# A gated mix of memory attention and GeGLU: the output and the other branch sent through DRAM scratches

## The chip, the cores and the metric

One core of a Trainium2 chip. The metric is the device time of one execution in microseconds, the median over the runs. TensorE (PE) multiplies, ScalarE (ACT), VectorE (DVE) and GpSimd (POOL) move and transform, SyncE (SP) issues nearly all DMAs, which sixteen DMA engines carry out.

## What is computed

Two branches over the same shape, 2048 rows of 640 columns in bf16, mixed by a gate computed from the first branch's input.

```python
def _A_ref(x, mem0, Wq, Wk, Wv, Wo, seg_len):      # 32 heads of 192, M = 8, seg_len = 32
    mem = mem0
    for s in range(n_seg):                          # 64 segments, one after the other
        xs = x[:, s*seg_len:(s+1)*seg_len, :]
        h = jnp.concatenate([mem, xs], axis=1)      # 40 rows
        q, k, v = (jnp.einsum('btd,dhe->bhte', h, W) for W in (Wq, Wk, Wv))
        p = _softmax(jnp.where(mask, q @ k.T * scale, -1e9))
        o = jnp.einsum('bhte,hed->btd', p @ v, Wo)
        mem = o[:, :M, :]                           # the next segment's memory
        outs.append(o[:, M:, :])

def _B_ref(x, w_gate, w_up, w_down):                # 640 -> 1536 -> 640
    return (gelu(x @ w_gate) * (x @ w_up)) @ w_down

g = sigmoid((A_x * gate_w).sum(-1))
out = g * _A_ref(...) + (1 - g) * _B_ref(A_x, ...)
```

## The kernel before

The kernel first computes the whole of the other branch (`_B_ref`) in four blocks of 512 rows, the feed-forward phase. `ffn_down` evacuates each 128 rows into a buffer `brow` and stores them in a DRAM tensor `b_scr` (L878), as rows of 640 columns. At the same time `x_stage` lays the transposed input out in DRAM, and the attention weights are loaded.

Then come the 64 segments in order, each an unrolled list of items (`PROG`, `PROG1`, `PROG3`): `("g", i, k)` are projections, `("tq", o)`/`("tk", o)` transposes, `("sc", o)`, `("ex", o)`, `("pt", o)` scores, softmax and its transposition, `("pv", o)` the product with V and `("wo", o, h)` the output projection. `o` is one of four octets of heads. The place `q = s % 4` of a segment in its group `g = s // 4` decides which list it takes. Every segment works on its 24 rows of x that have no part in the next memory together with the 8 rows of memory; the segment's last 8 rows, the "left" rows, are worked on for four segments at a time (`LQ`, `LK`, `Vl`, `Wb`).

The weights don't all fit. Thirteen pieces of Q, K and V (each 128 partitions of 3072 bytes) and three of Wo (3840 bytes) share their places with a partner: as soon as the first octet's piece was used, `swap_loads` issues the DMA (L635) for the partner that the last octet needs later in the same segment. The next segment goes over the octets in the other order, so every segment swaps once more.

All DMAs of the segment phase are in SP's one stream, in the order in which the items add them, and SP waits for a DMA's conditions before it goes on to the next. The ones that matter here:

- `out_store(s - 1)` (L1029) writes the mixed 32 partitions x 4 column blocks of the segment before, buffer `bz`, to the output. At place 0 it is added at `("g", 0, KT-2)`, ahead of the rest of the K swaps and of the V swaps; at the other places at `("g", 1, KT-1)`, behind the V swaps.
- `x_load(s + 1)` (L743) follows it at `("g", 1, KT-1)`.
- `bz_load(s)` (L1018), after `("wo", 0, 1)`, loads this segment's 32 rows of the other branch into the same buffer `bz`, as four column blocks of 160 columns one below the other. It waits for the output store's landing.
- `mix(s)` multiplies `bz` by one minus the gate on GpSimd (`mix1`, L1085), and VectorE adds the gated attention output (`mix2`, L1087).
- `stg_load` (L1005) brings the left rows' Q and K back from `left_qk_scratch` for the next segment, and one more swap, a Q piece, is added next to it after `("pv", 2)`.
- The left rows of the output and of the other branch have their own buffer `bzl`: `bzl_load` (L1024) and `outl_store` (L1072), once in a group and in eight DMAs each, four at `("g", 1, KT-1)` and four at `("pv", 2)`.

The patterns of the load and of the store put the column block first:

```python
e.dma_start(bz, b_scr[L * s:L * s + L, :].rearrange("t (j n) -> j t n", j=4))
e.dma_start(out2[L * s:L * s + L, :].rearrange("t (j n) -> j t n", j=4), bz)
```

The last segment has no `bz`; `end_load` reads its rows of `b_scr`, and `end_store` writes them.

Of the kernel before, what the change touches and what calls it, by code (L numbers as in the profile page):

```python
# [6 lines left out]
BF = mybir.dt.bfloat16  # L7
# [231 lines left out]
def _build(nc, A_x, A_mem0, A_Wq, A_Wk, A_Wv, A_Wo, seg_len, w_gate, w_up, w_down,  # L239
           gate_w, out, opts=None):  # L240
    opts = dict(opts or {})
    Bsz, S, Dm = A_x.shape
    M = A_mem0.shape[1]
    H, Dh = A_Wq.shape[1], A_Wq.shape[2]
    Df = w_gate.shape[1]
    L = int(seg_len)
    assert Bsz == 1 and M == 8 and L == 32 and Dh == 192
    assert Dm % 128 == 0 and H % 4 == 0 and S % 128 == 0 and Df % 128 == 0
    KT = Dm // 128
    DJ = Dm // 4  # L250
# [32 lines left out]
    g_scr = nc.dram_tensor("gate_scratch", (M, NSEG), F32, kind="Internal").ap()  # L283
# [154 lines left out]
    bz, bzl = [bview(wsB_off[nm], DJ * 2) for nm in ("bz", "bzl")]  # L438
# [8 lines left out]
    LROW = ((3, 4), (0, 3))  # L447
    r_bzlj = [[sreg(wsB_off["bzl"], DJ * 2, 32 * j, 32 * j + M), sreg(wsB_off["bzl"], DJ * 2, 32 * j + M, 32 * j + 32)] for j in range(4)]
# [3 lines left out]
    r_bz, r_bzl = [sreg(wsB_off[nm], DJ * 2) for nm in ("bz", "bzl")]  # L452
# [36 lines left out]
    brow = [bview(ffn_off["brow"] + b * Dm * 2, Dm * 2) for b in range(NBR)]  # L489
    r_brow = [sreg(ffn_off["brow"] + b * Dm * 2, Dm * 2) for b in range(NBR)]  # L490
# [183 lines left out]
    def load_residents(cls, pick=lambda key: True):  # L674
        for key in first:
# [7 lines left out]
           reads=[r_ident], writes=[r_ident])  # L683
# [10 lines left out]
    for i in range(2):  # L694
# [3 lines left out]
               reads=[r_elw], writes=[r_elw])  # L698
# [152 lines left out]
    def ffn_down(blk):  # L851
        n1 = min(Dm, 512)
        for a in range(FA):
            xb = 3 + 2 * (a % 2)
            yb = xb + 1
            wr = [r_ps[xb]] + ([r_ps[yb]] if Dm > 512 else [])
            fns = []
            for f in range(FT):
                if a == 0 and f == FT - 1:
                    S_.add("pe", fns, reads=[r_wd] + r_hT[:f], writes=wr, name="ffn down %d %d" % (blk, a))  # L860
                    fns = []
                fns.append(lambda e, f=f, a=a, xb=xb: e.matmul(ps[:, xb, 0:n1], hT_sb[:, f, a * 128:(a + 1) * 128], wd_sb[:, f, 0:n1],  # L862
                                                               start=(f == 0), stop=(f == FT - 1)))
                if Dm > 512:
                    fns.append(lambda e, f=f, a=a, yb=yb: e.matmul(ps[:, yb, 0:Dm - 512], hT_sb[:, f, a * 128:(a + 1) * 128], wd_sb[:, f, 512:Dm],
                                                                   start=(f == 0), stop=(f == FT - 1)))
            S_.add("pe", fns, reads=[r_wd] + r_hT, writes=wr, name="ffn down %d %d" % (blk, a))
            bs = a % NBR
            S_.add("act", lambda e, bs=bs, xb=xb: e.activation(out=brow[bs][:, 0:n1], in_=ps[:, xb, 0:n1], func=ACTF.Copy),
                   reads=[r_ps[xb]], writes=[r_brow[bs]], name="ffn b evac")  # L870
            if Dm > 512:
                S_.add("dve", lambda e, bs=bs, yb=yb: e.tensor_copy(out=brow[bs][:, 512:Dm], in_=ps[:, yb, 0:Dm - 512]),
                       reads=[r_ps[yb]], writes=[r_brow[bs]], name="ffn b evac2")
            if blk + 1 < NFB:
                for r in range(2 * a, min(2 * a + 2, NGR)):
                    gate_part(blk + 1, r)
            row0 = blk * FB + a * 128
            S_.add(AUXQ, lambda e, bs=bs, row0=row0: e.dma_start(b_scr[row0:row0 + 128, :], brow[bs]),  # L878
                   reads=[r_brow[bs]], writes=[Rg("dr", row0, row0 + 128)], dma_sem="bw%d" % bs, watch=True,
                   name="b store %d" % row0)  # L880

    warm(14)
    ffn_transposes(0)
# [3 lines left out]
    for blk in range(NFB):  # L887
        if blk:
            x_stage(blk)
        ffn_gu(blk)  # L890
        if blk == 0:
            chain_init()
        if blk + 1 < NFB:
            ffn_transposes(blk + 1)
        if blk + 2 < NFB:
            ffn_x_load(blk + 2)
        if blk + 1 == NFB:
            load_residents(1, lambda key: key not in loaded.values())
        ffn_down(blk)
        if blk + 2 == NFB:  # L900
            load_residents(1, lambda key: res_off[key] >= ffn_off["xr"] and res_off[key] + piece_size(key) <= ffn_off["xT"])
        if blk == 0:
            x_load(0)
            xl_load(0)
            xl_load(1)
            x_copy(0)
# [96 lines left out]
    def stg_load(s, h):  # L1003
        lo = (h + s) % 2 * 2
        S_.add(AUXQ, lambda e: e.dma_start(stg_half[h].rearrange("p (o w) -> p o w", o=2), qkl[NOCT * (s // 4) + lo:NOCT * (s // 4) + lo + 2].rearrange(  # L1005
            "o p (q w) -> p q o w", q=4)[:, s % 4]),
               reads=[Rg("qk", NSEG * i + s, NSEG * i + s + 1) for i in (lo, lo + 1)],
               writes=r_stgh[h], dma_sem="stg%d" % h, name="stg s%d %d" % (s, h))
# [6 lines left out]
               name="Kl s%d o%d" % (s, o))  # L1015

    def bz_load(s):
        S_.add(AUXQ, lambda e: e.dma_start(bz, b_scr[L * s:L * s + L, :].rearrange("t (j n) -> j t n", j=4)),  # L1018
               reads=[Rg("dr", 128 * (s // 4), 128 * (s // 4) + 128)], writes=[r_bz], dma_sem="bz", name="bz load s%d" % s)

    def bzl_load(g, js):
        for j in js:
            for n, (lo, hi) in enumerate(LROW):
                S_.add(AUXQ, lambda e, j=j, n=n, lo=lo, hi=hi: e.dma_start(  # L1024
                    bzl[32 * j + M * n:32 * j + M * (n + hi - lo)], rows(b_scr, g)[1][lo:hi, :, DJ * j:DJ * (j + 1)]),
                    reads=[Rg("dr", 128 * g, 128 * g + 128)], writes=[r_bzlj[j][n]], dma_sem="bzl%d" % (2 * j + n), name="bzl load g%d" % g)

    def out_store(s):
        S_.add(AUXQ, lambda e: e.dma_start(out2[L * s:L * s + L, :].rearrange("t (j n) -> j t n", j=4), bz),  # L1029
               reads=[r_bz], writes=[Rg("do%d" % j, s, s + 1) for j in range(4)], dma_sem="outs", watch=True, name="out s%d" % s)  # L1030

    assert r_XLg[1].lo == r_XLg[0].hi and KT * 64 == DJ * 2
    bzx = bview(wsA_off["XLg"], 4 * DJ)
# [4 lines left out]
    r_gx = sreg(wsA_off["xs"], 8)  # L1038

    def end_rows(ap, h, x, lo, hi):  # L1040
        v = ap[L * lo:L * hi, 2 * DJ * h:2 * DJ * (h + 1)]
        return v[0:XA] if x == 0 else v.rearrange("(s t) d -> s t d", t=L)[:, XA:L, :]

    def end_load():
# [24 lines left out]
    def outl_store(g, js):  # L1069
        for j in js:  # L1070
            for n, (lo, hi) in enumerate(LROW):
                S_.add(AUXQ, lambda e, j=j, n=n, lo=lo, hi=hi: e.dma_start(  # L1072
                    rows(out2, g)[1][lo:hi, :, DJ * j:DJ * (j + 1)], bzl[32 * j + M * n:32 * j + M * (n + hi - lo)]),
                    reads=[r_bzlj[j][n]], writes=[Rg("do%d" % j, 4 * g + lo, 4 * g + hi)], dma_sem="outl%d" % (2 * j + n), watch=True, name="outl g%d" % g)

    omg = fview(wsA_off["stats"] + 64, 8)
    r_omg = sreg(wsA_off["stats"] + 64, 8)
# [384 lines left out]
    def segment(s):  # L1462
# [3 lines left out]
        for n, item in enumerate(PROGS[q]):  # L1466
# [210 lines left out]
```

## Time and profile before

| | |
|---|---|
| Median of 3 runs | 1651.54 us (1647.38 to 1653.57) |
| Span of the profiled execution | 2114.2 us |
| The profiled execution's own time | the page gives none beside the span |
| Mean granted TensorE clock in it | 0.654 |
| Busy PE / DVE / ACT / POOL | 2098.0 / 1005.8 / 792.9 / 553.3 us |
| DMA packets | 275415, 499.28 MB |

The profiled execution is longer than the timed ones. Windows are in microseconds from the first instruction; the feed-forward phase lasts to about 264 us, the segments from there on. The DMA share is the mean over the sixteen engines. A row of the timeline has the start, the duration, the engine and the line; SPq is SP's stream of DMA issues, whose duration is the issue's and not the transfer's.

### The profile page before, as it was taken

Reading aid. Unit: us, or ns where it says so; the run is one execution under the profiler, and the core shown is the slowest. Engines: PE = TensorE matmul, PEld = TensorE weight load, DVE = VectorE, ACT = ScalarE, POOL = GpSimd, SP = SyncE. Lnnn points to the kernel's source line nnn. Section 1 sums busy time; section 2 is a strip of 40 time slices with the busy share of each in tenths; the row PEclk is TensorE's granted clock in tenths of the full one; section 3 lists DMA queues with packets and bytes.
Section 4 is the critical chain, followed back from the end, with each engine's and each line's share of the span. In section 5 each row is a group of like instructions: output and inputs, shape, how many; then the busy total and the mean of one; then the engine's idle time right before and its main releaser. Section 6 shows DMA issues by size and latency. Waiting matters only on the chain.

```text
span 2114.2 us, 75845 instructions
## 1 busy us (share of the span) xinstructions
PE 2098.0 (99%) x37107; PEld 958.1 (45%) x28147; DVE 1005.8 (48%) x3039; ACT 792.9 (38%) x1890; POOL 553.3 (26%) x1625
## 2 busy tenths in 40 slices
PE   9999999999999999999999999999999999999997
PEld 3444344444444444444444444444444444444444
DVE  4233254554545454545545454545455454545453
ACT  1111244343434343444434343434444343434342
POOL 1000023232232223232222323232322223222332
PEclk6666666666666666666666666666666666666666
DMA  9612577776768777677767677776777676777775
GB/s 319 182 33 57 184 268 260 248 270 232 253 219 275 244 258 241 227 255 254 274 233 249 221 268 249 255 251 225 248 256 270 239 258 212 261 256 249 254 264 174
DMA packets 275415, 499.28 MB, mean 236 GB/s; under 512 B 121119, under 2 KB 136327, under 8 KB 275079
## 3 DMA queue, kind: packets, MB, share of 16 engines
q1 hardware_dynamic: 271000, 491.30, 68.8%
q8 instruction: 255, 4.18, 0.8%
q10 hardware_dynamic: 4079, 3.14, 0.5%
q14 instruction: 81, 0.66, 0.1%
HBM read 473.25 MB, written 21.09 MB: 234 GB/s over the span
## 4 chain that ended last, share of the span: by engine, by line
PE 99%; DMA 0%; DVE 0%; SPq 0%; POOL 0%; ACT 0%; issue 0%; ACTq 0%; POOLq 0%; DVEq 0%
PE ps L226 26%; PE ps L1138 25%; PE ps L1338 9%; PE ps L1383 8%; PE ps L1282 4%; PE ps L930 4%; PE ps L839 4%; PE ps L836 4%; PE ps L862 3%; PE ps L1364 3%; PE ps L1187 2%; PE ps L1284 2%; PE ps L234 1%; PE ps L1195 1%; PE ps L971 1%; PE ps L1254 1%
## 5 line engine op out<-in xcount | busy, mean ns | idle before, releaser
L226 PE MATMUL ps<-arena 128*32 128x384 bf16 x8960 | 887.8, 430 | 0.4 <-ACT arena L1159 0.4
L1138 PE MATMUL ps<-arena 128*32 128x384 bf16 x8640 | 857.5, 420 | 2.0 <-DVE arena L1583 2.0
L1138 PEld LDWEIGHTS ps<-arena 128*32 128x32 bf16 x8640 | 303.3, 117 | 525.3 <-issue 379.7
L1176 DVE STREAM_TRANSPOSE arena<-arena 128x384 bf16<-128x384 bf16 x512 | 276.5, 562 | 144.1 <-ACT arena L1159 144.1
L1159 ACT ACTIVATE arena<-ps 128x384 bf16<-128x384 f32 x512 | 230.0, 491 | 160.1 <-PE ps L1138 160.1
L1214 DVE TENSOR_REDUCE arena<-ps 104x4 f32<-104x160 f32 x256 | 83.0, 324 | 340.2 <-PE ps L1202 340.2
L1338 PE MATMUL ps<-arena 128*32 128x320 bf16 x3456 | 241.0, 404 | 0.0
L1012 POOL COPY arena<-arena 128x96 bf16<-128x96 bf16 x256 | 70.2, 274 | 475.3 <-PE ps L1202 311.4
L1267 ACT ACTIVATE arena<-ps 128x448 bf16<-128x448 f32 x192 | 104.4, 544 | 237.7 <-PE ps L1254 233.3
L1179 POOL COPY arena<-arena 64x160 bf16<-64x160 bf16 x256 | 81.9, 320 | 385.5 <-DVE arena L1176 384.3
L1162 ACT ACTIVATE arena<-ps 128x384 bf16<-128x384 f32 x256 | 125.2, 489 | 128.1 <-PE ps L1138 127.5
L1383 PE MATMUL ps<-arena 128*64 128x320 bf16 x1536 | 169.6, 387 | 0.0
L1226 ACT ACTIVATE ps<-ps 104x160 f32<-104x160 f32 x256 | 74.8, 292 | 239.5 <-DVE ps L1216 239.5
L1320 ACT ACTIVATE arena<-ps 128x480 bf16<-128x480 f32 x192 | 109.5, 570 | 93.8 <-PE ps L1284 85.7
L930 PE MATMUL ps<-arena 128*32 128x384 bf16 x1280 | 142.5, 408 | 0.0
L1338 PEld LDWEIGHTS ps<-arena 128*32 128x32 bf16 x3456 | 113.3, 129 | 56.9 <-ACT arena L1261 18.1
L1282 PE MATMUL ps<-arena 128*64 128x160 bf16 x1536 | 135.2, 263 | 0.0
L1284 PE MATMUL ps<-arena 128*64 128x64 bf16 x1536 | 128.6, 225 | 0.0
L1228 DVE TENSOR_REDUCE arena<-ps 104x4 f32<-104x160 f32 x256 | 81.8, 319 | 88.4 <-ACT ps L1226 87.4
L1383 PEld LDWEIGHTS ps<-arena 128*64 128x64 bf16 x1536 | 93.2, 127 | 49.4 <-issue 9.6
L1282 PEld LDWEIGHTS ps<-arena 128*64 128x64 bf16 x1536 | 94.1, 126 | 42.8 <-ACT arena L1159 23.0
L1411 ACT ACTIVATE arena<-ps 128x384 bf16<-128x384 f32 x120 | 57.3, 491 | 123.9 <-DVE arena L1580 74.0
(102 smaller groups left out, 2518.2 us busy)
## 6 DMA issues: line engine op xcount, KB each, us to landing
arena<-in_A_Wk_dram SPq DMA_DIRECT2D x335, 384.0 KB, 5.8
arena<-in_A_Wv_dram SPq DMA_DIRECT2D x335, 384.0 KB, 8.4
arena<-in_A_Wo_dram SPq DMA_DIRECT2D x205, 480.0 KB, 4.3
arena<-in_A_Wq_dram SPq DMA_DIRECT2D x209, 384.0 KB, 4.8
arena<-left_qk_scratch SPq DMA_DIRECT2D x126, 96.0 KB, 3.9
left_qk_scratch<-arena SPq DMA_DIRECT2D x49, 192.0 KB, 4.6
left_qk_scratch<-arena SPq DMA_DIRECT2D x30, 96.0 KB, 3.7
ffn_b_scratch<-arena ACTq DMA_DIRECT2D x16, 160.0 KB, 2.3
```

The source lines that it names most:

```text
L226: return e.add_instruction(mybir.InstMatmult(name=nm, start_tensor_calc=like["start"], stop_tensor_calc=stop, tile_size=(128, 32), tile_po ...
L930: fns.append(lambda e, outp=outp, rhs=rhs, j=j: e.matmul(outp, lhs, rhs, start=(k == 0), stop=(k == KT - 1), tile_position=(0, 32 * j)))
L1138: fns.append(lambda e, outp=outp, rhs=rhs, j=j: e.matmul(outp, lhs, rhs, start=(k == 0), stop=(k == KT - 1), tile_position=(0, 32 * j)))
L1159: S_.add("act", lambda e, m=m, bk=bk: e.activation(out=rows_sb[m], in_=ps[:, bk, 0:384], func=ACTF.Copy), reads=[r_ps[bk]], writes=[r_rows ...
L1162: S_.add("act", lambda e, i=i, bk=bk: e.activation(out=v_sb[i % NVB].rearrange("p (c n) -> p c n", c=3), in_=ps[:, bk, 0:384].rearrange("p ...
L1176: S_.add("dve", lambda e: e.transpose(out=dst[:, :, 0:L], in_=rows_sb[m].rearrange("p (c r) -> p c r", r=L)), reads=[r_rows[m]], writes=[r ...
L1267: S_.add("act", lambda e: e.activation(out=PT, in_=ps[:, bank, 0:PTW + 128], func=ACTF.Copy), reads=[r_ps[bank]], writes=[r_PT], name="pT ...
L1282: return [lambda e: e.matmul(full, v[:, e0:e0 + 64], PTm[:, i], start=True, stop=False, tile_position=(0, 64 * i), skip_group_check=True), ...
L1284: lambda e: e.matmul(part, vl[:, e0:e0 + 64], PTl[:, i], start=False, stop=True, tile_position=(0, 64 * i), skip_group_check=True)]
L1320: S_.add("act", lambda e: e.activation(out=apx(u[:, 0, 0, :], [[rs, na], [3 * rs, 4], [1, R]]), in_=ps[:, A, 0:na * W].rearrange("p (c t r ...
L1338: fns.append(lambda e, i=i, t=t, j=j, gv=gv: e.matmul(ps[32 * j:32 * j + 32, bank, 0:2 * DJ].rearrange("p (h n) -> p h n", h=2), lhs2[i], ...
L1383: S_.add("pe", [lambda e, i=i, g_=g_, c=c, p=p, u=u: e.matmul(ps[64 * i:64 * i + 64, LB, 0:2 * DJ], u[:, c, :], g_[:, c, 2 * DJ * i:2 * DJ ...
```

## The change

The other branch goes to DRAM twice removed from its rows: `ffn_down` stores each 128 rows in four DMAs into `b2_scr`, ordered by segment, column block and row, so that `bz_load` reads 128 consecutive rows of 160 columns. The left rows are gathered from there into `b3_scr` by copies from DRAM to DRAM (`b_left_copy`), so that `bzl_load` is one DMA. Only the last 128 rows still go into `b_scr`, for the end. In the last block these stores are in SP's stream instead of ACT's.

The output goes the same way back: `out_store` and `outl_store` write `o2_scr` and `o3_scr`; `out_left` copies the left rows into `o2_scr`, and `out_copy` copies sixteen segments at a time, one column block per DMA, to the output. These copies are added one in a segment behind `("pv", 2)`, in the eight segments after every sixteenth; the last twelve segments that go this way are copied in segments 61 and 62, four DMAs each. Segments 60 to 62 store to the output directly, and the end is as before.

At place 0, `out_store` moves to where the other places have it, behind the V swaps.

```diff
-    b_scr = nc.dram_tensor("ffn_b_scratch", (S, Dm), BF, kind="Internal").ap()
+    b_scr = nc.dram_tensor("ffn_b_scratch", (128, Dm), BF, kind="Internal").ap()
+    b2_scr, o2_scr = [nc.dram_tensor(nm, (NSEG, 4, L, Dm // 4), BF, kind="Internal").ap() for nm in ("b_segments", "out_segments")]
+    b3_scr, o3_scr = [nc.dram_tensor(nm, (NG, 4, 4, M * (Dm // 4)), BF, kind="Internal").ap() for nm in ("b_left", "out_left")]
...
-            S_.add(AUXQ, lambda e, bs=bs, row0=row0: e.dma_start(b_scr[row0:row0 + 128, :], brow[bs]),
...
+            for q in range(4):
+                S_.add("sp" if blk + 1 == NFB else AUXQ, lambda e, bs=bs, row0=row0, q=q: e.dma_start(
+                    b2_scr[row0 // L + q].rearrange("j t n -> t j n"), brow[bs][L * q:L * q + L].rearrange("t (j n) -> t j n", j=4)),
...
+            if row0 + 128 == S:
+                S_.add("sp", lambda e, bs=bs: e.dma_start(b_scr, brow[bs]), reads=[r_brow[bs]], writes=[Rg("dr", S - 128, S)],
+                       dma_sem="bwl", name="b store")
+
+    def seg_left(scr, lo, hi, q):
+        return scr[lo:hi].rearrange("(g q) j t n -> q g j (t n)", q=4)[q][:, :, XA * DJ:L * DJ]
+
+    def b_left_copy(half, q):
+        g0, g1 = 8 * half, 8 * half + 8
+        S_.add("sp", lambda e: e.dma_start(b3_scr[g0:g1, :, (q + 1) % 4], seg_left(b2_scr, 4 * g0, 4 * g1, q)),
...
     def bz_load(s):
-        S_.add(AUXQ, lambda e: e.dma_start(bz, b_scr[L * s:L * s + L, :].rearrange("t (j n) -> j t n", j=4)),
+        S_.add(AUXQ, lambda e: e.dma_start(bz, b2_scr[s].rearrange("j t n -> (j t) n")),
...
+    def bzl_load(g):
+        S_.add(AUXQ, lambda e: e.dma_start(bzl, b3_scr[g].rearrange("j q (t n) -> (j q t) n", n=DJ)),
...
     def out_store(s):
+        if s < NSEG - 4:
+            S_.add(AUXQ, lambda e: e.dma_start(o2_scr[s].rearrange("j t n -> (j t) n"), bz), reads=[r_bz],
+                   writes=[Rg("o2", s, s + 1)], dma_sem="outs", name="out s%d" % s)
+            return
...
+    def outl_store(g):
+        S_.add(AUXQ, lambda e: e.dma_start(o3_scr[g].rearrange("j q (t n) -> (j q t) n", n=DJ), bzl), reads=[r_bzl],
+               writes=[Rg("o3", g, g + 1)], dma_sem="outl", name="outl g%d" % g)
+
+    def out_left(lo, hi, q):
+        g0, g1 = lo // 4, hi // 4
+        form = "g j x -> g j x" if g1 - g0 == 4 else "g j x -> j g x"
+        S_.add(AUXQ, lambda e: e.dma_start(seg_left(o2_scr, lo, hi, q).rearrange(form), o3_scr[g0:g1, :, (q + 1) % 4].rearrange(form)),
+               reads=[Rg("o3", g0, g1)], writes=[Rg("o2", lo, hi)], dma_sem="outf%d" % q, name="out left s%d" % lo)
+
+    def out_copy(lo, hi, j):
+        form = "s t n -> s t n" if hi - lo == 16 else "s t n -> t s n"
+        S_.add(AUXQ, lambda e: e.dma_start(
+            out2[L * lo:L * hi, DJ * j:DJ * (j + 1)].rearrange("(s t) n -> s t n", t=L).rearrange(form),
+            o2_scr[lo:hi].rearrange("s j t n -> j s t n")[j].rearrange(form)),
...
-                if s and q == 0:
-                    out_store(s - 1)
             if item == ("g", 1, KT - 1):
-                if q:
+                if s:
                     out_store(s - 1)
...
+                if 3 <= s <= 6:
+                    b_left_copy(1, s - 3)
+                lo, i = s // 16 * 16 - 16, s % 16 - 1
+                if lo >= 0 and 0 <= i < 8:
+                    (out_left if i < 4 else out_copy)(lo, lo + 16, i % 4)
+                if s in (NSEG - 3, NSEG - 2):
+                    for i in range(4):
+                        (out_left if s == NSEG - 3 else out_copy)(NSEG - 16, NSEG - 4, i)
...
-            if item in (("g", 1, KT - 1), ("pv", NOCT - 2)):
-                js = (0, 1) if item[0] == "g" else (2, 3)
-                if q == 0 and g > 0:
-                    outl_store(g - 1, js)
-                if q == 2 and g + 1 < NG:
-                    bzl_load(g, js)
+            if item == ("pv", NOCT - 2) and q == 0 and g > 0:
+                outl_store(g - 1)
+            if item == ("pv", NOCT - 2) and q == 2 and g + 1 < NG:
+                bzl_load(g)
```

The copies of the first half of the left rows, `b_left_copy(0, q)`, are added in the feed-forward phase after the third block's `ffn_gu`.

More of the change, by code (lines that the diff above doesn't have):

```diff
@@ L877, in ffn_down @@
             row0 = blk * FB + a * 128
-            S_.add(AUXQ, lambda e, bs=bs, row0=row0: e.dma_start(b_scr[row0:row0 + 128, :], brow[bs]),
-                   reads=[r_brow[bs]], writes=[Rg("dr", row0, row0 + 128)], dma_sem="bw%d" % bs, watch=True,
-                   name="b store %d" % row0)
+            for q in range(4):
+                S_.add("sp" if blk + 1 == NFB else AUXQ, lambda e, bs=bs, row0=row0, q=q: e.dma_start(
+                    b2_scr[row0 // L + q].rearrange("j t n -> t j n"), brow[bs][L * q:L * q + L].rearrange("t (j n) -> t j n", j=4)),
+                    reads=[r_brow[bs]], writes=[Rg("d2", row0 // L + q, row0 // L + q + 1)], dma_sem="bw%d_%d" % (bs, q),
+                    name="b store %d" % row0)
+            if row0 + 128 == S:
[6 more added lines that the diff above has]
+        S_.add("sp", lambda e: e.dma_start(b3_scr[g0:g1, :, (q + 1) % 4], seg_left(b2_scr, 4 * g0, 4 * g1, q)),
+               reads=[Rg("d2", 4 * g0, 4 * g1)], writes=[Rg("d3", 4 * half + q, 4 * half + q + 1)],
+               dma_sem="bl%d" % q, name="b left copy %d %d" % (half, q))
     warm(14)
@@ L890, in _build @@
         ffn_gu(blk)
+        if blk == 2:
+            for q in range(4):
+                b_left_copy(0, q)
         if blk == 0:
@@ L1017, in bz_load @@
     def bz_load(s):
[L1018 to L1026, printed above, removed]
+        S_.add(AUXQ, lambda e: e.dma_start(bz, b2_scr[s].rearrange("j t n -> (j t) n")),
+               reads=[Rg("d2", s, s + 1)], writes=[r_bz], dma_sem="bz", name="bz load s%d" % s)
+    def bzl_load(g):
+        S_.add(AUXQ, lambda e: e.dma_start(bzl, b3_scr[g].rearrange("j q (t n) -> (j q t) n", n=DJ)),
+               reads=[Rg("d3", 4 * (g // 8), 4 * (g // 8) + 4)], writes=[r_bzl], dma_sem="bzl", name="bzl load g%d" % g)
     def out_store(s):
+        if s < NSEG - 4:
+            S_.add(AUXQ, lambda e: e.dma_start(o2_scr[s].rearrange("j t n -> (j t) n"), bz), reads=[r_bz],
+                   writes=[Rg("o2", s, s + 1)], dma_sem="outs", name="out s%d" % s)
+            return
         S_.add(AUXQ, lambda e: e.dma_start(out2[L * s:L * s + L, :].rearrange("t (j n) -> j t n", j=4), bz),
-               reads=[r_bz], writes=[Rg("do%d" % j, s, s + 1) for j in range(4)], dma_sem="outs", watch=True, name="out s%d" % s)
+               reads=[r_bz], writes=[Rg("do%d" % j, s, s + 1) for j in range(4)], dma_sem="oute", watch=True, name="out s%d" % s)
     assert r_XLg[1].lo == r_XLg[0].hi and KT * 64 == DJ * 2
@@ L1040, in end_rows @@
     def end_rows(ap, h, x, lo, hi):
-        v = ap[L * lo:L * hi, 2 * DJ * h:2 * DJ * (h + 1)]
+        off = S - ap.shape[0]
+        v = ap[L * lo - off:L * hi - off, 2 * DJ * h:2 * DJ * (h + 1)]
         return v[0:XA] if x == 0 else v.rearrange("(s t) d -> s t d", t=L)[:, XA:L, :]
@@ L1067, in end_store @@
                    dma_sem="outx%d" % i, watch=True, name="out end")
[L1069 to L1074, printed above, removed]
+    def outl_store(g):
[11 more added lines that the diff above has]
+            o2_scr[lo:hi].rearrange("s j t n -> j s t n")[j].rearrange(form)),
+            reads=[Rg("o2", lo, hi)], writes=[Rg("do%d" % j, lo, hi)], dma_sem="outm%d" % j, watch=True, name="out copy s%d" % lo)
     omg = fview(wsA_off["stats"] + 64, 8)
```

## The prediction

> **What bounds the kernel now.** I read the page first: engine shares, the slices, the chain that ended last.
>
> ```profile
> span 2114.2 us, 75845 instructions
> PE 2098.0 (99%) x37107; PEld 958.1 (45%) x28147; DVE 1005.8 (48%) x3039; ACT 792.9 (38%) x1890; POOL 553.3 (26%) x1625
> ...
> PEclk6666666666666666666666666666666666666666
> DMA  9612577776768777677767677776777676777775
> ...
> DMA packets 275415, 499.28 MB, mean 236 GB/s; under 512 B 121119, under 2 KB 136327, under 8 KB 275079
> ...
> q10 hardware_dynamic: 4079, 3.14, 0.5%
> ...
> PE 99%; DMA 0%; DVE 0%; SPq 0%; POOL 0%; ACT 0%; issue 0%; ACTq 0%; POOLq 0%; DVEq 0%
> ```
>
> In this execution TensorE is the bound and nothing else is: 2098.0 of 2114.2 us, at a granted clock of about 0.65. The page gives no time for this execution beyond its span. The timed runs have a median of 1651.54 us, less than TensorE's busy time here, so they did not run at this clock. The sum must go by a rescaled trace: what TensorE paces shrinks with the clock, what the DMA engines and SP's issues pace does not. So I read the stretches: the segment phase, the feed-forward phase, then one period of four segments (places 0 to 3) and pieces of it.
>
> ```profile
> core 0: us, PE busy (x) PEld busy (x) DVE busy (x) ACT busy (x) POOL busy (x), PEclk, DMA share, GB/s
> 264.00:2092.00 1828.00, 1824.72 (x35732) 845.79 (x26928) 912.98 (x2860) 742.17 (x1799) 530.57 (x1569) 0.65 0.73 250
> 0.00:264.00 264.00, 261.63 (x1237) 104.52 (x1073) 90.08 (x169) 47.48 (x83) 20.20 (x51) 0.66 0.52 155
> 939.79:1055.78 115.99, 115.99 (x2266) 53.87 (x1704) 57.86 (x181) 47.06 (x115) 33.59 (x100) 0.65 0.73 249
> 1010.00:1026.70 16.70, 16.70 (x335) 6.06 (x206) 8.46 (x25) 7.63 (x18) 3.80 (x15) 0.65 0.85 303
> 1026.70:1036.70 10.00, 10.00 (x233) 6.50 (x210) 5.50 (x21) 4.11 (x10) 4.13 (x11) 0.65 0.66 216
> 1052.70:1066.70 14.00, 14.00 (x210) 8.86 (x206) 4.81 (x19) 4.38 (x12) 5.36 (x12) 0.65 0.48 152
> ```
>
> A period is 115.99 us; 1828.00 us hold 15.76 of them. The mean DMA engine is busy 0.73 x 115.99 = 84.7 us of it. At full clock TensorE would need 115.99 x 0.65 = 75.4 us, less than the DMA engines' 84.7. Scaling the phases alike, 264 x 0.66 + 1828 x 0.65 + 22.2 x 0.65 = 174 + 1188 + 14 = 1376 us is TensorE's time at full clock. Two readings of 1651 us remain. Either TensorE still sets it, at a clock of 1376 / 1651 = 0.83. Or the clock is full and 275 us are waits for DMAs: (1651 - 174 - 14) / 15.76 = 92.8 us a period, 17.4 more than TensorE needs. I take the second as likelier: DMA work fills 84.7 us of a period on the mean engine, and the engines that carry more come closer to 92.8; the first needs a clock that no row shows.
>
> The Trainium skill, "TensorE: Matmul & The Clock Gate" (Part 1), says of the peak-current limiter that one or two busy cores never trip it. By that rule one core runs at full clock and the second reading holds; the 0.65 above, with one core, does not agree with it, so it settles nothing.
>
> **Which engines are loaded unevenly.** The list of DMA issues:
>
> ```profile
> arena<-left_qk_scratch SPq DMA_DIRECT2D x126, 96.0 KB, 3.9
> ...
> ffn_b_scratch<-arena ACTq DMA_DIRECT2D x16, 160.0 KB, 2.3
> arena<-ffn_b_scratch SPq DMA_DIRECT2D x63, 40.0 KB
> out_dram<-arena SPq DMA_DIRECT2D x63, 40.0 KB
> ...
> arena<-x_scratch SPq DMA_DIRECT2D x63, 30.0 KB, 8.7
> arena<-ffn_b_scratch SPq DMA_DIRECT2D x60, 2.5 KB
> arena<-ffn_b_scratch SPq DMA_DIRECT2D x60, 7.5 KB
> ```
>
> The lines whose transfers have four column blocks outermost in their pattern (and the small left ones) show no time to landing; those with 128 partitions outermost show one. Their landings were not counted as sixteen. The Trainium skill, "DMA: Bandwidth & Descriptors" (on why a DMA increments its semaphore by 16), says that a DMA runs on the largest number up to 16 that divides both outermost dimensions, and on the lowest-numbered engines; by that these run on four. The missing landings agree. I work with four.
>
> **The chain that would be late at full clock.** In each segment SP issues 13 swaps, then the output store of the segment before (L1029), then x; later the load of the other branch (L1018) into the same buffer, which must wait for that store; then Pool's mix (L1085) waits for that load. Place 0 differs: its store goes out ahead of the V swaps.
>
> ```profile
> 950.81 1.01 SPq L635 DMA_DIRECT2D arena<-in_A_Wk_dram  x2
> 952.65 0.57 SPq L1029 DMA_DIRECT2D out_dram<-arena  x1
> 955.30 2.90 SPq L635 DMA_DIRECT2D arena<-in_A_Wv_dram  x5
> 972.15 0.59 SPq L1018 DMA_DIRECT2D arena<-ffn_b_scratch  x1
> 980.88 1.04 SPq L635 DMA_DIRECT2D arena<-in_A_Wk_dram  x2
> 988.44 0.59 SPq L1029 DMA_DIRECT2D out_dram<-arena  x1
> 1002.96 0.58 SPq L1018 DMA_DIRECT2D arena<-ffn_b_scratch  x1
> 1010.04 1.05 SPq L635 DMA_DIRECT2D arena<-in_A_Wk_dram  x2
> 1017.35 0.59 SPq L1029 DMA_DIRECT2D out_dram<-arena  x1
> 1029.03 0.58 SPq L1018 DMA_DIRECT2D arena<-ffn_b_scratch  x1
> 1032.26 2.37 SPq L1024 DMA_DIRECT2D arena<-ffn_b_scratch  x4
> 1036.71 1.04 SPq L635 DMA_DIRECT2D arena<-in_A_Wk_dram  x2
> 1044.01 0.61 SPq L1029 DMA_DIRECT2D out_dram<-arena  x1
> 1054.33 0.57 SPq L1018 DMA_DIRECT2D arena<-ffn_b_scratch  x1
> 978.71 0.69 POOL L1085 TENSOR_SCALAR arena<-arena 128x160 bf16<-128x160 bf16 x1 [0.17 <-POOL arena L1080]
> 1008.18 0.69 POOL L1085 TENSOR_SCALAR arena<-arena 128x160 bf16<-128x160 bf16 x1 [0.17 <-POOL arena L1080]
> 1034.85 0.68 POOL L1085 TENSOR_SCALAR arena<-arena 128x160 bf16<-128x160 bf16 x1 [0.17 <-POOL arena L1080]
> 1062.73 0.69 POOL L1085 TENSOR_SCALAR arena<-arena 128x160 bf16<-128x160 bf16 x1
> ```
>
> Landings, as estimates: x, issued right behind the store, lands after 8.7 us, so the store takes about 9.0; the row of left_qk_scratch, issued right behind the load, gives the load about 3.9. Counted from the first swap, at full clock:
> - Place 1: store issued at 7.6, landed at 16.6. The load's turn comes at (1002.96 - 980.88) x 0.65 = 14.4, so SP stands until 16.6; the load lands at 20.5, the mix's turn is (1008.18 - 980.88) x 0.65 = 17.7: late by 2.8 us.
> - Place 2: 7.3 + 9.0 + 3.9 = 20.2 against 24.81 x 0.65 = 16.1: late by 4.1.
> - Place 3: 20.2 against 26.02 x 0.65 = 16.9: late by 3.3.
> - Place 0: the store is early; the load's turn is 13.9, it lands at 17.8, the mix's turn is 18.1: in time.
>
> That is 10.2 of the 17.4 us. The rest I put to the swaps themselves, which the change leaves.
>
> **The change, part by part.** The price of one 320-byte packet (160 columns of bf16; 40 KB are 128 of them) has no row. From below: in 1010.00 to 1026.70 an engine moves 303 / 0.85 / 16 = 22.3 GB/s, which makes 14 ns. From above: the Activation queue's packets of 770 bytes on average cost 0.005 x 16 x 2114.2 us / 4079 = 41 ns. I take the middle, 28 ns.
>
> *Load and store on sixteen engines.* 128 packets each over 16 engines instead of 4: 8 instead of 32 on an engine, twice 24 x 28 ns = 1.34 us off the late chain at places 1 to 3: -4.0 us a period (-2.0 to -5.9). The lateness (2.8, 4.1, 3.3) is larger each time, so all of it counts.
>
> *The store of place 0 behind the V swaps.* It leaves at 958.20, 7.4 after the start, lands at 7.4 + 9.0 - 0.7 = 15.7, behind the load's turn at 13.9. SP stands there 1.8 us with the loads of left_qk_scratch and one Q swap queued behind; the load lands at 15.7 + 3.9 - 0.7 = 18.9 against 18.1: +0.8 us. The V swaps come 32 x 28 ns = 0.9 us earlier on the four engines, but I find them not late, so nothing for that (0 to +1.5).
>
> *The left rows* go in one DMA each way instead of eight. Four of L1024 take SP 2.37 us just ahead of the next segment's swaps, where one would take about 0.6: 1.8 us, which counts only as far as SP is the last; -0.5 (0 to -1.8).
>
> *Copies.* A period has one output copy of 512 packets, 32 on each engine, and one left copy of 16 packets on four engines, each in SP's order ahead of the next segment's swaps. DRAM to DRAM has no row: from 28 ns to 56 ns (read and written as two of the above), 0.9 to 1.8 us, plus 4 left packets of 2560 bytes at 22.3 GB/s, 4 x 0.12 = 0.5 us. The stretches there have DMA shares of 0.66 and 0.48, at full clock 1.0 and 0.74, so about half is hidden: +1.2 us (0 to +2.3).
>
> *The feed-forward phase.* 64 stores instead of 16; the Activation queue is far from full (47.48 of 264 us) and DMA has idle slices there: nothing. In the last block they stand on SP: 17 issues, the last five (3 us) ahead of the gate loads and the last resident weights: about 3 us once if that cover fails.
>
> *The end.* Four left copies write one region, so each waits for the one before: three waits of about 3.9 us, of which TensorE covers some 8 us: 4 us. Four copies of 384 packets ahead of the last segment's swaps: 96 x 56 ns = 5 us. With the 3 above: +12 us once (0 to 12).
>
> Sum: -4.0 + 0.8 - 0.5 + 1.2 = -2.5 us a period, x 15.76 = -39, + 12 = -27: 1651 - 27 = **1624 us**. Ends: with 41 ns, the left rows' full 1.8 and copies free, (-5.9 + 0.8 - 1.8) x 15.76 = -109: 1542. With 14 ns and the dear ends, (-2.0 + 1.5 + 2.3) x 15.76 + 12 = +40: 1691. All ends at once are unlikely.
>
> **The rivals.** *TensorE bound at 0.83.* For it: the profiled execution has no DMA wait at all. Against it: above. The periods keep their length; only the one-off 0 to 5 us show: 1651 to 1656, no difference, and I take 1652.
>
> *Slower: a DRAM-to-DRAM packet is dear.* Without the copy the period gains 4.0 - 0.8 + 0.5 = 3.7 us, less the left copy's 0.5. The output copy puts 32 packets on every engine ahead of swaps. From 3.2 us / 32 = 100 ns a packet it takes the gain, if none is hidden. At the 138 ns of a 3072-byte packet (3072 / 22.3) it costs 4.4 us: +1.2 x 15.76 + 12 = +31: 1682 us. For it: nothing of this kind was in the trace. Against it: the 41 ns row. The Trainium skill, "DMA: Bandwidth & Descriptors" (Specifications), says that under 512 bytes a DMA engine does a read-modify-write, which would speak for it; no row here shows it for such a copy.
>
> *It doesn't do what it says*: the new patterns still run on few engines. Then the copies and the ends stand alone: 1651 + (0.8 + 1.2) x 15.76 + 12 = 1695 us.
>
> **Chances.** Forecast 0.55, TensorE bound 0.18, dear packet 0.21, not as said 0.06. A measurement of this kernel tells about 0.5% (8 us) from no change. The forecast's case ends near no change at its upper side, but the bound by swaps could also free more; I leave 0.56 for faster, 0.18 for the same, 0.26 for slower. The range reaches from 1572 (most of the way to the best end) to 1672, which leaves out the dearest copies and the last rival. Within the likeliest case alone: 1580 to 1645.
>
> **What would show it.** In the changed profile the lines of bz loads and output stores should have times to landing; L1024's groups of four should be single issues; at a clock of 0.65 the span should stay within 10 us of 2114, since TensorE covers all of it. If a profile at a higher clock shows no TensorE wait behind Pool's mix or the swaps, the chain is wrong; if the copies' issues are followed by late swaps, the dear packet is right; if the timed median stays within 8 us, TensorE sets it.

## The result: slower by 0.9%

| | median | runs | ratio to before (95% interval) |
|---|---|---|---|
| before | 1652.55 us | 6 | |
| changed | 1664.32 us | 6 | 1.0087 (1.0062 to 1.0111) |

The change costs 0.9%, 12 us by these medians and 14 by the ratio, where a gain of 27 was forecast. That 1664 us lies within 1572 to 1672 is luck: the range was wide enough to hold a loss as well. The execution profiled took 1663.57 us, 2.1 more than its span, at a granted clock of 0.994. The profile shown before the change had 0.654, so its lines are no measure beside these. Run e0 below is the kernel before once more; its profiled execution has 0.992 and takes part in all comparisons from here on.

The head of the page of the changed kernel:

```profile
span 1661.5 us, 75708 instructions
PE 1568.0 (94%) x37107; PEld 773.2 (47%) x28147; DVE 1000.3 (60%) x3039; ACT 785.1 (47%) x1890; POOL 552.4 (33%) x1625
...
PEclk9999999999999999999999999999999999999998
DMA  9925898899889899999989898999888898999885
...
DMA packets 291667, 503.18 MB, mean 303 GB/s; under 512 B 138795, under 2 KB 152083, under 8 KB 291331
```

and of the kernel before at full clock (e0):

```profile
span 1656.0 us, 75828 instructions
PE 1569.1 (95%) x37090; PEld 774.2 (47%) x28147; DVE 998.3 (60%) x3039; ACT 784.6 (47%) x1890; POOL 549.6 (33%) x1625
...
DMA packets 275415, 499.28 MB, mean 301 GB/s; under 512 B 121119, under 2 KB 136327, under 8 KB 275079
```

The engines do the same work in the same time; 16,252 packets and 3.9 MB were added. TensorE was not freed of waits. Its busy time at full clock is 1569 us, not 1376, and in e0 it is idle for 87 us in all.

The DMA issues of the changed kernel that answer to those shown of before:

```profile
arena<-left_qk_scratch SPq DMA_DIRECT2D x126, 96.0 KB, 3.9
...
arena<-b_segments SPq DMA_DIRECT2D x63, 40.0 KB, 4.2
out_segments<-arena SPq DMA_DIRECT2D x60, 40.0 KB, 9.4
...
out_dram<-out_segments SPq DMA_DIRECT2D x12, 160.0 KB, 4.6
arena<-x_scratch SPq DMA_DIRECT2D x63, 30.0 KB, 8.9
...
arena<-b_left SPq DMA_DIRECT2D x15, 40.0 KB, 3.4
out_left<-arena SPq DMA_DIRECT2D x15, 40.0 KB, 4.1
```

Load and store have times to landing now, so the spreading is real. But the store takes 9.4 us, not the 9.0 - 0.7 of the prediction, and the load 4.2, not 3.9 - 0.7. x, right behind the store, lands after 8.9 us against 8.7 in e0.

The waits on the path that was to be shortened, SP's at the bz load and GpSimd's at the mix, first in e0, then in the changed kernel (who waited for what: us in total, times, longest):

```profile
SPq L1018 <- DMA out_dram<-arena: 55.8, 32, 3.9
...
POOL arena L1085 <- DMA arena<-ffn_b_scratch: 26.5, 37, 2.4
```

```profile
SPq L1037 <- DMA out_segments<-arena: 87.9, 42, 3.9
...
SPq L1097 <- DMA out_segments<-out_left: 6.7, 3, 3.4
...
POOL arena L1116 <- DMA arena<-b_segments: 39.9, 45, 2.9
```

Both waits grew. Next comes the steady state. The bz load comes once in a segment, so its first and last start give the length of 62 segments. The rows are of e0, the changed kernel, and e4, which has no swaps (below):

```profile
L1018 SPq DMA_DIRECT2D arena<-ffn_b_scratch x63: 548/582/932, 193.8 to 1612.3; - x63
```

```profile
L1037 SPq DMA_DIRECT2D arena<-b_segments x63: 326/327/1385, 199.2 to 1619.9; - x63
```

```profile
L1020 SPq DMA_DIRECT2D arena<-ffn_b_scratch x63: 554/579/611, 183.0 to 1541.6; - x63
```

That is 22.88, 22.91 and 21.91 us a segment. Single executions of one kernel scatter by half a per cent, so such rows say where time may be, and the ratios say how much there is.

### The profile page after: what moved, and what is told of

Its sections match the earlier page's. It is cut to its first block, busy times and chain, and to the rows that moved or that the text cites. A ratio compares the mean times of both kernels' runs of the same rounds, so it can differ in the third digit from the quotient of the medians.

```text
span 1661.5 us, 75708 instructions
## 1 busy us (share of the span) xinstructions
PE 1568.0 (94%) x37107; PEld 773.2 (47%) x28147; DVE 1000.3 (60%) x3039; ACT 785.1 (47%) x1890; POOL 552.4 (33%) x1625
## 5 line engine op out<-in xcount | busy, mean ns | idle before, releaser
L1169 PE MATMUL ps<-arena 128*32 128x384 bf16 x8640 | 644.0, 329 | 19.7 <-DMA arena<-in_A_Wv_dram 9.0
L226 PE MATMUL ps<-arena 128*32 128x384 bf16 x8960 | 646.4, 327 | 4.5 <-issue 1.2
L1169 PEld LDWEIGHTS ps<-arena 128*32 128x32 bf16 x8640 | 227.5, 96 | 397.9 <-issue 263.9
L1369 PE MATMUL ps<-arena 128*32 128x320 bf16 x3456 | 183.2, 300 | 10.3 <-issue 5.9
L1031 POOL COPY arena<-arena 128x96 bf16<-128x96 bf16 x256 | 69.7, 272 | 246.1 <-PE ps L1233 160.7
L1414 PE MATMUL ps<-arena 128*64 128x320 bf16 x1536 | 122.9, 304 | 1.3 <-DMA arena<-in_A_Wo_dram 0.8
L1313 PE MATMUL ps<-arena 128*64 128x160 bf16 x1536 | 117.6, 240 | 5.8 <-ACT arena L1190 3.4
L1369 PEld LDWEIGHTS ps<-arena 128*32 128x32 bf16 x3456 | 88.2, 96 | 51.3 <-ACT arena L1292 18.4
L949 PE MATMUL ps<-arena 128*32 128x384 bf16 x1280 | 108.8, 328 | 0.3 <-issue 0.3
L1359 POOL COPY arena<-arena 128x96 bf16<-128x96 bf16 x192 | 51.7, 269 | 160.6 <-ACT arena L1341 93.8
L1315 PE MATMUL ps<-arena 128*64 128x64 bf16 x1536 | 103.7, 193 | 0.9 <-issue 0.9
L1313 PEld LDWEIGHTS ps<-arena 128*64 128x64 bf16 x1536 | 81.4, 109 | 41.8 <-ACT arena L1193 14.4
```

The lines of the kernel that those rows point to most:

```text
L226: return e.add_instruction(mybir.InstMatmult(name=nm, start_tensor_calc=like["start"], stop_tensor_calc=stop, tile_size=(128, 32), tile_po ...
L949: fns.append(lambda e, outp=outp, rhs=rhs, j=j: e.matmul(outp, lhs, rhs, start=(k == 0), stop=(k == KT - 1), tile_position=(0, 32 * j)))
L1169: fns.append(lambda e, outp=outp, rhs=rhs, j=j: e.matmul(outp, lhs, rhs, start=(k == 0), stop=(k == KT - 1), tile_position=(0, 32 * j)))
L1313: return [lambda e: e.matmul(full, v[:, e0:e0 + 64], PTm[:, i], start=True, stop=False, tile_position=(0, 64 * i), skip_group_check=True), ...
L1315: lambda e: e.matmul(part, vl[:, e0:e0 + 64], PTl[:, i], start=False, stop=True, tile_position=(0, 64 * i), skip_group_check=True)]
L1369: fns.append(lambda e, i=i, t=t, j=j, gv=gv: e.matmul(ps[32 * j:32 * j + 32, bank, 0:2 * DJ].rearrange("p (h n) -> p h n", h=2), lhs2[i], ...
```

## Experiments

Each ratio below is to the runs of the kernel before that were made beside that run. Their median was 1648.93 us for e0 to e3, 1653.84 for e4 to e7 and 1652.36 for e8 to e11, so runs are compared with each other by their ratios; 0.1% is 1.65 us.

**e0: the kernel before, for its profile at full clock.** No edit.

> The kernel before, unchanged, for a profile at the clock of the timed runs (the changed kernel's profile has a granted clock of 0.99). All theories: about 1652 us. The chain theory of the prediction says that Pool's mix (L1085) waits for the bz load at places 1 to 3 by 3 to 4 us each and that the period of four segments is about 92 us; if the mix waits for less than 1 us a time, that chain was not what filled the period. The ends theory (one-off work at the end costs the time) says that the last segment takes about 25 us here, against 34.5 us in the changed kernel.

Measured: 1650.45 us. The mix waits 26.5 us in 37 times, 0.7 us each, not 3 to 4: the chain was not what filled the period. The period is 4 x 22.88 = 91.5 us, as worked out. The ends theory missed on the last segment: from the first swap of segment 63 to the end of the span it takes 35.4 us in e0 (from 1620.56) and 36.2 in the changed kernel (from 1625.33), not 25 against 34.5. A segment at place 2, in e0:

```profile
777.59 0.82 SPq L635 DMA_DIRECT2D arena<-in_A_Wk_dram  x2
...
784.89 0.60 SPq L1029 DMA_DIRECT2D out_dram<-arena  x1
...
793.84 0.58 SPq L1018 DMA_DIRECT2D arena<-ffn_b_scratch  x1
...
798.24 0.68 POOL L1085 TENSOR_SCALAR arena<-arena 128x160 bf16<-128x160 bf16 x1 [0.81 <-DMA arena<-ffn_b_scratch]
```

The store is issued 7.3 us after the first swap and the load 16.3 after it, both as worked out. But the mix's own turn is 798.24 - 0.81 - 777.59 = 19.8 us after it, where the rescaled trace put 16.1: between the two profiles it went from 24.6 to 19.8 us, to 0.80 and not to 0.65. So the load is 0.8 us late and not 4.1.

**e1: the changed kernel, place 0's store back ahead of the swaps.**

```diff
+                if s and q == 0:
+                    out_store(s - 1)
             if item == ("g", 1, KT - 1):
-                if s:
+                if q:
                     out_store(s - 1)
...
```

> The changed kernel with the output store of place 0 back ahead of the K and V swaps. Theory 'place 0' (the store behind the V swaps makes SP stand at the bz load): faster than the changed kernel by 10 us or more, 1654 us or less. Theory 'copies' (DRAM to DRAM copies ahead of swaps): 1664 us, within 4. Theory 'ends' (work added once at the end): 1664 us, within 4.

Measured: 1660.1 us, 1.0067 of before (1.0044 to 1.0090). The changed kernel's interval overlaps this one: the move costs 0.2% or nothing here, not the 10 us of 'place 0'. The other two theories allowed 1660. SP's wait at the load stays: 82.2 us in 38 times, so the move is not what made it grow.

**e2: the kernel before with the move alone.** The same edit the other way round.

> The kernel before with only the output store of place 0 moved behind the V swaps, on four engines as before. Theory 'place 0': slower than before by 10 us or more, 1662 us or more. Theories 'copies' and 'ends': within 4 us of 1652.

Measured: 1725.3 us, 1.0473 (1.0446 to 1.0501). 'Place 0' had the direction right, and none had the size, 4.7% or 78 us. SP's own waits show where it goes:

```profile
SPq L1072 <- DMA out_dram<-arena: 111.6, 15, 8.2
SPq L1018 <- DMA out_dram<-arena: 56.1, 33, 3.2
```

The second row is as in e0. The first is new: 15 times 7.4 us in front of the left rows' store. It stands right behind the output store and its region overlaps that store's, so it waits for a landing behind the whole V queue; Wo swaps and the bz load are queued behind it. TensorE's waits for Wo swaps grow from 4.7 to 53.8 us. Its busy time grows too, from 1569.1 to 1591.0 us: in all five of these executions the granted clock is 0.975 to 0.979, where the full-clock executions of the other kernels have 0.99 or more.

**e8: the move alone, with the left stores later.** The edit of e2, and this:

```diff
+            if item == ("pv", NOCT - 2) and q == 0 and g > 0:
+                outl_store(g - 1, (0, 1, 2, 3))
             if item in (("g", 1, KT - 1), ("pv", NOCT - 2)):
                 js = (0, 1) if item[0] == "g" else (2, 3)
-                if q == 0 and g > 0:
-                    outl_store(g - 1, js)
...
```

> The kernel before with the output store of place 0 behind the V swaps (alone 1725 us), and all eight left stores of the group behind ('pv', 2) instead of four of them right behind the output store. Theory 'same rows' (SP stands because the left store writes rows that the output store before it is noted to write, 111.6 us in 15 waits): the waits go and the time is 1655 us or less. Theory 'late bz' (the store's own landing, seen by the bz load, cost the 75 us): 1700 us or more.

Measured: 1656.7 us, 1.0041 (1.0019 to 1.0064). The waits at L1072 are gone from the list, and all but 0.4 of the 4.7% with them: 'same rows' holds, though the median is 1.7 us above what it allowed. The granted clock is back at 0.993 to 0.998. In the changed kernel the left store goes to its own scratch and at `("pv", 2)`, and its list of waits has no such row.

**e3: the changed kernel without output copies.** The calls of `out_left` and `out_copy` are removed.

> The changed kernel without its copies from the output scratches to the output and without the left rows' copies between the scratches; the output rows of segments 0 to 59 are not written. Theory 'copies': 25 us or more below the changed kernel, spread over the segments that had copies, 1640 us or less. Theory 'ends': about 10 us below it, all of it in segments 61 to 63, about 1654 us. Theory 'place 0': 1664 us, within 5.

Measured: 1654.54 us, 1.0026 (1.0005 to 1.0047). That is 0.6%, about 10 us, below the changed kernel: 'ends' has the size, 'copies' does not. What is left, sixteen engines and the move with no output copy to pay for, is still not faster than before.

**e6: the changed kernel without the end copies alone.** The calls in segments 61 and 62 are removed, the 24 earlier ones stay.

> The changed kernel without the four left copies in segment 61 and the four output copies in segment 62 (the rows of segments 48 to 59 are not written); the copies between segments 17 and 56 stay. Theory 'ends': nearly all of what the copies cost goes, 1656 us or less, as without any copy (1654.5 us). Theory 'copies everywhere': about 1661 us, since 24 of the 32 places with copies are left.

Measured: 1657.92 us, 1.0027 (1.0012 to 1.0042). The median is 2 us above what 'ends' allowed, but the runs of before beside it are 5 us above those beside e3; the ratio is the same as e3's. So the copies in the middle cost nothing that can be measured, and those at the end cost about 0.6%. SP's stream of the changed kernel there:

```profile
1594.20 9.11 SPq L1097 DMA_DIRECT2D out_segments<-out_left  x4
1603.35 0.45 SPq L1024 DMA_DIRECT2D arena<-left_qk_scratch  x1
1603.85 0.94 SPq L637 DMA_DIRECT2D arena<-in_A_Wk_dram  x2
...
1621.69 3.26 SPq L1102 DMA_DIRECT2D out_dram<-out_segments  x4
1625.33 2.12 SPq L637 DMA_DIRECT2D arena<-in_A_Wk_dram  x2
```

Four left copies hold SP for 9.11 us, since each is noted as writing the region of the one before; four output copies hold it for another 3.26, and the next segment's first swaps stand behind both.

**e9: the changed kernel with its ends mended.**

```diff
-               reads=[Rg("o3", g0, g1)], writes=[Rg("o2", lo, hi)], ...
+               reads=[Rg("o3", g0, g1)], writes=[Rg("o2", i, i + 1) for i in range(lo + q, hi, 4)], ...
...
-                if s in (NSEG - 3, NSEG - 2):
-                    for i in range(4):
-                        (out_left if s == NSEG - 3 else out_copy)(NSEG - 16, NSEG - 4, i)
+                if s == NSEG - 3:
+                    for i in range(4):
+                        out_left(NSEG - 16, NSEG - 4, i)
...
             if item == ("g", 1, KT - 1):
...
+                if s + 1 == NSEG:
+                    for i in range(4):
+                        out_copy(NSEG - 16, NSEG - 4, i)
```

> The changed kernel, complete, with its four left copies of segment 61 noted as writing different rows, so that none waits for another, and its last four output copies moved from segment 62 to segment 63 behind the V swaps, where no Q, K or V swap follows. Theory 'ends': as without these copies, 1655 to 1659 us. Theory 'bytes' (their traffic costs wherever it stands): 1664 us, within 3.

Measured: 1659.37 us, 1.0045 (1.0017 to 1.0072). The median is just above what 'ends' allowed and below 'bytes'; the interval reaches over e6 and over the changed kernel, so this run does not decide. e6 shows that it is the copies at the end that cost; whether by SP's standing in them or by their traffic is not shown.

**e7: the other branch's side alone.** The stores into the segment scratch, the left copies and the two loads of the change; the output side and the order as before.

> The kernel before with the other branch's side alone changed: stores of 320-byte rows into the segment scratch, left copies, one load of the left rows, bz load on sixteen engines; the output side as before, the store of place 0 too. Theory 'off the path': 1649 us, within 4. Theory 'feed-forward' (the stores on SP in the last block and the copies there delay the start of the segments): 1653 us or more, with the first segments later. The prediction's arithmetic (half of 4.0 us a period): 1617 us.

Measured: 1657.19 us, 1.0023 (1.0003 to 1.0043). The prediction's 1617 is out. The time is within the bounds of 'feed-forward', but those were set beside 1649 us, and the runs of before beside e7 have 1653.84, so the time alone does not tell it from 'off the path'. The starts of all profiles do. Where the feed-forward phase is as before (e0, e2, e5, e8, e10), the first bz load starts at 190.7 to 193.8 us; where it has the change's stores and copies (the changed kernel, e1, e3, e6, e7, e9, e11), at 196.5 to 199.2. By the means that is 5.6 us later, 0.3%, and e7's segments are as long as before's (22.94 against 22.88). So the start of the segments is enough to account for e7's 0.2%. SP's stream there, in e0 and then in the changed kernel:

```profile
157.07 1.41 SPq L792 DMA_DIRECT2D arena<-gate_scratch  x2
168.38 2.39 SPq L635 DMA_DIRECT2D arena<-in_A_Wo_dram  x5
```

```profile
162.14 11.51 SPq L881 DMA_DIRECT2D b_segments<-arena  x16
...
174.16 1.14 SPq L794 DMA_DIRECT2D arena<-gate_scratch  x2
175.35 3.28 SPq L637 DMA_DIRECT2D arena<-in_A_Wo_dram  x5
```

The stores of the last block hold SP for 11.51 us, and the gate loads and the resident weights stand behind them. That this is what delays the start fits, but no run moves these stores back.

**e5: neither load nor store.** The bz loads of segments 1 to 59 and the output stores of 0 to 59 are left out of the kernel before.

> The kernel before without the bz loads of segments 1 to 59 and without the output stores of segments 0 to 59; the mixing runs on what stands in the buffer. This is the most that any speeding up of the two can bring. The prediction's chain (mix late by 3 to 4 us at three places in four): 1550 us or less. Theory 'off the path' (the mix has slack, and the swaps' landings don't move): 1640 us or more.

Measured: 1651.7 us, 0.9983 (0.9964 to 1.0001). With both transfers gone altogether the kernel gains 0.2% or nothing. By the interval, no way of speeding these two up can bring more than 0.4%, whatever engines they run on.

**e4: no swaps.** `load_piece` returns before its DMA where the name begins with "swap".

> The kernel before without the swaps of Q, K, V and Wo pieces (the pieces loaded first are used throughout); everything else is issued and computed as before. It gives the time without the weights' DMA chain. Theory 'swaps' (the landing of the swaps, about 16.5 us after a segment's start at every place in both kernels, sets the 23 us of a segment): a segment falls to about 20 us or less and the whole to below 1500 us. Theory 'compute' (TensorE and the chain through the other engines fill the 23 us): a segment stays above 22 us and the whole above 1600 us.

Measured: 1587.4 us, 0.9597 (0.9563 to 0.9631); 21.91 us a segment by the rows above. Both theories missed: 'swaps' asked for less than 1500, 'compute' for over 1600. But it lies near 'compute': 96% of the time is there without the swaps, and all that the swaps cost is about 66 us.

**e10 and e11: a wait that both kernels have.** e0's list of waits ends TensorE's longest one with a copy on GpSimd, and GpSimd stands for the last rows' loads:

```profile
PE ps L1202 <- POOL arena L1296: 9.0, 1, 9.0
POOL arena L1057 <- DMA arena<-ffn_b_scratch: 8.6, 1, 8.6
```

The edit is the same in both; e11 has that of e9 as well.

```diff
                 if s + 1 < NSEG:
                     bz_load(s)
+                    if s + 2 == NSEG:
+                        end_load()
                 else:
-                    end_load()
                     end_gates()
...
```

> The kernel before with the six loads for the last rows issued in segment 62 instead of 63. In the profile at full clock GpSimd's mix of these rows waits 8.58 us for them, and TensorE waits 9.0 us for a copy queued behind it. If that wait is on the path: about 1641 us, 8 us below the kernel before. If the last segment has another chain as late: 1647 us or more.

Measured: 1643.43 us, 0.9943 (0.9920 to 0.9965), and in the list of waits:

```profile
PE ps L1202 <- POOL arena L1296: 1.0, 1, 1.0
POOL arena L1057 <- POOL arena L1055: 0.3, 1, 0.3
```

The wait was on the path. This version is 0.6% below the kernel before and 1.4% below the changed one.

> The changed kernel with both: the ends mended and the last rows' loads a segment earlier. If both act: 8 us below the kernel with the ends mended alone, 1647 to 1651 us. If the scratches are worth anything once the ends cost nothing: below the kernel before with the early loads, under 1640 us.

Measured: 1649.29 us, 0.9990 (0.9963 to 1.0017). It gains on e9 what e10 gains on before, about 0.6%: both act. It is not under 1640: with the same repair the scratches are 0.5% behind the kernel without them, though the two intervals just meet. Their later start remains (first bz load at 197.2 us against 192.6 in e10).

## Why the prediction was wrong

**The clock was right, TensorE's time at it was wrong.** This is the step that failed. The second reading of 1651 us had full clock, and e0 shows 0.992. But the 1376 us, and the 75.4 us of a period, came from multiplying TensorE's stretches by the granted clock. The segments of e0:

```profile
190.00:1610.00 1420.00, 1356.46 (x35026) 670.32 (x26382) 885.60 (x2803) 719.59 (x1765) 516.50 (x1535) 1.00 0.89 315
```

TensorE is busy for 1356.46 of 1420.00 us, which is 87.4 of the 91.5 us of a period. The period's length had been worked out well (92.8); what fills it had not. Over the whole kernel TensorE's busy time fell from 2098.0 to 1569.1 us, to 0.75, where the clock would make 0.654 / 0.992 = 0.66. So the 275 us of waits for DMAs were at most the 87 us that TensorE is idle in e0, and without swaps the kernel gains only 66, with TensorE still busy for 1545.6 us (e4). The -2.5 us a period was priced on a gap that isn't there.

Which matmuls didn't follow the clock can be seen by their shapes, first in the profile of before, then in e0 (busy time and the mean ns of one):

```profile
L836 PE MATMUL ps<-arena 128*128 128x512 bf16 x240 | 87.4, 513 | 0.6 <-DMA arena<-in_B_w_gate_dram 0.4 <-DVE arena L825 0.2
L226 PE MATMUL ps<-arena 128*32 128x384 bf16 x8960 | 887.8, 430 | 0.4 <-ACT arena L1159 0.4
L1187 PE MATMUL ps<-arena 128*40 128x160 bf16 x512 | 64.0, 247 | 0.0
```

```profile
L836 PE MATMUL ps<-arena 128*128 128x512 bf16 x235 | 59.2, 379 | 1.3 <-DMA arena<-in_B_w_gate_dram 1.0 <-DVE arena L825 0.2
L226 PE MATMUL ps<-arena 128*32 128x384 bf16 x8960 | 646.7, 327 | 5.3 <-issue 1.0 <-ACT arena L1159 1.0 <-DMA arena<-in_A_Wq_dram 0.6
L1187 PE MATMUL ps<-arena 128*40 128x160 bf16 x512 | 81.2, 247 | 4.5 <-POOL arena L1179 3.7
```

By busy time the wide matmuls of the feed-forward phase went to 0.68 (5 of their 240 records are missing), the projections in tiles of 32 columns to 0.73, and the matmul that opens the scores (L1187) did not shrink at all: its mean is 247 ns in both. Why a shape follows the clock or not is not shown.

**The late mix.** With the work ahead of it slower than worked out, the mix's own turn is later, and the lateness of 2.8, 4.1 and 3.3 us became 0.7 us on average where it waits at all. e5 bounds what its removal could bring to 0.4%. (Of the 13 swaps that the prediction puts ahead of the store, 12 stand there and one comes after `("pv", 2)`; no sum rests on it.)

**-4.0 us a period for sixteen engines.** The count of packets was right, the landing did not follow it. By the updates of the store's semaphore (means over segments 8 to 59, places 1 to 3) it lands 8.5 us after its issue in e0 and 9.1 to 9.4 in the changed kernel; e1, with the old order, has 9.1 to 9.5. In e0 four updates come between 7.7 and 8.5 us, behind one at 1.0: four engines, as the prediction took. On sixteen, thirteen updates come between 7.0 and 8.2 us and the last three by 9.1 to 9.4. So most engines are done earlier, but the landing waits for the slowest of them. The load went from 4.4 to 4.7 us by place to 3.9 to 4.9. For the store the term has the other sign: SP waits 32 us longer at the load in all, and 13 of them reach the mix; what that costs is too small to show in e3. The price of 28 ns a packet was not the fault: the records of 320-byte packets have a median of 20 ns in both kernels.

**+0.8 us a period for the move.** e1 makes it 0.2% with overlapping intervals, a few us instead of 13. The region that store and left store share was not seen; in this change it does no harm, alone it costs 4.7%.

**-0.5 us for the left rows, +1.2 for the copies.** No run has the left rows alone. The copies' term took the upper end of its own bounds (half of 1.4 to 2.3 is 0.7 to 1.2); e3 and e6 differ by nothing, so the middle's copies are covered. The slower rival, the dear DRAM-to-DRAM packet, falls with that, and the trace agrees: while the output copies run, the 320-byte packets have a median of 20 ns, not 100 or more.

**+12 us for the end.** The size holds: the end copies cost about 10 us by e3 and e6, where 9 were worked out, and the start of the segments 5.6, where 3 were. Together they make up the loss of about 14. The three waits of the left copies are there, in SP's 9.11 us. The TensorE-bound rival had the steady state right, with the wrong clock, and took these one-off costs for covered.

What stays open: whether the end copies cost by SP's order or by their traffic, what in the feed-forward phase delays the start, why the short matmuls don't follow the clock, and whether the move costs anything in the changed kernel.

## What to carry to other kernels

A profile at a lower clock can't simply be rescaled by the clock: first get one at the clock of the timed runs, or run the kernel without the transfers in question, which bounds any gain from them in one number. Before a transfer is made faster, ask what waits for it and with how much slack; spreading it over more engines also makes it wait for more of them. When a store is moved in an in-order stream, look at every later entry that shares its region: it waits there too. Compare where the phases start as well: a one-off delay shows in every profile before it shows in a time.

## What the runs showed of the hardware

One core's executions had granted clocks of 0.654 (span 2114.2 us) and of 0.992 (1656.0 us) for the same kernel; TensorE's busy time at the higher clock was 0.75 of that at the lower, and by shape of matmul between 0.68 and no less at all. In the kernel whose SP stands for 111.6 us at the left stores the granted clock was 0.975 to 0.979 in every execution, and 0.993 to 0.998 once that wait was gone (e2, e8).

A store of 128 packets of 320 bytes behind a full queue landed 8.5 us after its issue on four engines and 9.1 to 9.4 on sixteen. DRAM-to-DRAM copies of 512 packets of 320 bytes landed in 4.6 us in the middle of the segments, about as long as a 40 KB load from DRAM to SBUF (4.2 us).
